# Dense layer of an attention, expert and dense kernel: the matmuls of its two products alternate in threes

## The chip, the cores and the metric

The kernel runs on one core of a Trainium2 chip. The metric is the device time of one execution in microseconds (us), as the median of several runs. The core has a matrix engine (TensorE, "PE" in the profile, with its weight loads as "PEld"), a vector engine (VectorE, "DVE"), a scalar engine (ScalarE, "ACT"), GpSimd ("POOL") and a queue that starts DMAs (SyncE, "SP"). Each engine runs its own instructions in program order and waits on semaphores for the others.

## The reference

The kernel computes three layers after one another; only the last one is touched by the change.

```python
def reference(**kwargs):
    ...
    attn_out = _attn_ref(**attn_kwargs)          # clustered attention
    ...
    x = _moe_ref(x=x, **moe_kwargs)              # 1536 tokens, one of 8 experts each
    return _moe2_ref(x=x, **moe2_kwargs)         # the dense layer

def _moe2_ref(x, w_in, w_out) -> np.ndarray:
    h = x @ w_in                                 # (1536, 512) @ (512, 2048)
    g = h * (1.0 / (1.0 + np.exp(-1.702 * h)))
    return (g @ w_out).astype(np.float32)        # (1536, 2048) @ (2048, 512)
```

## The kernel before

Attention fills the first 280 us, the experts the time up to about 490 us, the dense layer the rest. Every operand of the dense layer is held as a high and a low part, and each product of two blocks is made of three matmuls: high by high, high by low, low by high.

The dense layer is cut into 48 groups, numbered `g` in the list `seq`. A group is one block of 128 hidden columns for one block of 512 tokens. The order is: two halves of the hidden columns (`fh`), three token blocks (`tb`) in each, eight groups in each of these. Two products belong to a group:

- The first product, here called in(g), is the function `dense_in`. It runs over four slices `k` of the 512 model columns with three matmuls each (L1084, L1085, L1086). All twelve matmuls have 512 columns and add into one PSUM buffer `ph` (there are four of them, `ps_h`). The moving operands are `yth` and `ytl`, the experts' results; the weights come from `w`.
- The second product, here called out(g), is `dense_out`. It runs over four blocks `m` of 128 model columns with three matmuls each (L1176 and L1177 read `gh`, L1178 reads `gl`), 512 columns wide, and adds into four PSUM buffers `py`, one for each `m`, which stay open over eight groups.

Between the two, `dense_h` makes g out of h: ACT takes the sigmoid of `ph` into `sg` (L1160), DVE multiplies (L1161), ACT rounds to the high part `gh` (L1164) and DVE subtracts to get the low part `gl` (L1167). There are three buffers each of `gh` and `gl`, and one `sg`.

The order of the instructions is written out by hand (`tc.manual_schedule`). The last loop of the kernel makes one step for each g. A step issues, in this order: the twelve matmuls of in(g); the sigmoid and the multiply of g; the twelve matmuls of out(g-2), block by block; after the last group of eight, `dense_store` for each block (an ACT copy L1183 in the first half, a DVE add L1185 and an output DMA from POOL in the second); the rounding to `gh`; two pieces of `dense_step`; the subtraction to `gl`; the remaining pieces of `dense_step`. `dense_step` converts the weights of later groups from 64-bit to two parts: L842 and L857 on ACT, L843, L846, L849, L852 on DVE, L858 on POOL. in(0) has already been issued in the experts' loop. So TensorE starts the layer with in(1), in(2), out(0), in(3), out(1).

Of the kernel before, what the change touches and what calls it, by code (L numbers as in the profile page):

```python
# [9 lines left out]
F32 = mybir.dt.float32  # L10
# [35 lines left out]
def attention_moe_ffn(ctx: ExitStack, tc: tile.TileContext, q, k, v, centroids, w_gate, w_og, w1, w2, w_in, w_out, out):  # L46
# [3 lines left out]
    def f32(ap):  # L50
        return ap.bitcast(F32)
# [14 lines left out]
    def scatter_id(b, j):  # L66
        x = nc.gpsimd.indirect_dma_start(
            out=idd[:, :], out_offset=bass.IndirectOffsetOnAxis(ap=ci[:, b, j:j + 1], axis=0),
            in_=tok[:, b, j:j + 1], in_offset=None).ins
        nc.gpsimd.engine_nop()  # L70
        tc.declare_no_dep(x, group="ids", reason="every token has a place of its own")
        tc.add_to_no_dep_group("ids", x)
        ids.append(x.name)
# [604 lines left out]
    def place_ids():  # L678

        nc.vector.tensor_tensor(eoff, off, ebase, op=ALU.subtract)  # L680
        for b in range(B):
            t1 = const.tile([128, T, E], F32, name=f"t1{b}")
            t2 = const.tile([128, T], F32, name=f"t2{b}")
            nc.vector.tensor_tensor(t1, roh[b], eoff[:, None, :].to_broadcast([128, T, E]), op=ALU.mult)
            nc.vector.tensor_reduce(t2, t1, op=ALU.add, axis=AX.X)
            nc.vector.tensor_tensor(ci[:, b], t2, place[b], op=ALU.add)
# [80 lines left out]
    def need(x, names):  # L767
        for nm in names:
            tc.add_manual_dep(x, nm, DATA_DEP, reason="all of them scattered")
# [7 lines left out]
    ps_h = ctx.enter_context(tc.tile_pool(name="ps_h", reuse_waits="tile", bufs=4, space=PSUM))  # L777
# [84 lines left out]
    def wa(key, part, k, i):  # L862
        return pairs[key]["w", 0][:, part].rearrange("p (k f) -> p k f", k=4)[:, k, i * 128:(i + 1) * 128]
# [54 lines left out]
    def win_h(d, key, i, defer=False):  # L918
        n = d["n"]
        ph = ps_h.tile([128, 512], F32, name="ph", tag="ph")  # L920
        for k in range(4):
            product(ph, n, wa(key, 0, k, i), wa(key, 1, k, i), d["t"][:, k], k == 0, k == 3)
        ht = hp.tile([128, 2 * CAP], F32R, name="ht", tag="ht")[:, :2 * n]
        lo, hi = ht[:, 0:n], ht[:, n:]
        t = ph[:, :n]
        if n <= 256:

            total(ph, n, t)
        nc.scalar.activation(hi, t, AF.Relu)

        def rest():
            nc.vector.scalar_tensor_tensor(lo, t, 0.0, f32(hi), op0=ALU.max, op1=ALU.subtract)
        if defer:
            return ht, rest
        rest()
        return ht
# [117 lines left out]
    def dense_step(upto):  # L1054
        while dl["done"] < min(upto, 20 * (DFF // 256)):
            if dl["done"] % (20 // QN) == 0:
                c, g = units[dl["split"]]
                dl["split"] += 1
                if wide:
                    new = wide_stages(c, g)  # L1060
                    if todo:
                        todo.appendleft(new.pop(0))
                    todo.extend(new)
                else:
                    todo.append(lambda: split_pair(("d", 0, c), g, dense_pool(c)))
                    todo.extend([None] * 9)
            f = todo.popleft()
            if f:
                f()
            dl["done"] += 1  # L1070
            if dl["done"] % (20 // QN) == 0:
                dense_load(dl["split"] + 2)


    seq = [(fh, tb, c, i) for fh in range(2) for tb in range(NT // 512) for c in range(4 * fh, 4 * fh + 4) for i in range(2)]
    ahead = {}

    def dense_in(g):
        _, tb, c, i = seq[g]
        key = ("d", 0, c)  # L1080
        ph = ps_h.tile([128, 512], F32, name="ph", tag="ph")
        cs = slice(tb * 512, tb * 512 + 512)
        for k in range(4):
            nc.tensor.matmul(ph, wa(key, 0, k, i), yth[:, k, cs], start=(k == 0), stop=False)  # L1084
            nc.tensor.matmul(ph, wa(key, 0, k, i), ytl[:, k, cs], start=False, stop=False)  # L1085
            nc.tensor.matmul(ph, wa(key, 1, k, i), yth[:, k, cs], start=False, stop=(k == 3))  # L1086
        ahead[g] = ph

    with tc.manual_schedule():
        win_start(0, True)  # L1090
# [22 lines left out]
        for g in range(G + 2):  # L1113
# [10 lines left out]
            if g < G:  # L1124
                ht, low = win_h(wins[e], ("e", e, c // 2), c % 2, True)
                hq.append((g, ht))
            if g == G + 1:
                dense_in(0)
            if g >= 2:
                g0, ht = hq.popleft()  # L1130
# [25 lines left out]
    def dense_h(ph):  # L1156
        gh = gp.tile([128, 512], F32R, name="gh", tag="gh")
        gl = gp.tile([128, 512], F32R, name="gl", tag="gl")
        sg = gp.tile([128, 512], F32, name="sg", tag="sg", bufs=1)
        nc.scalar.activation(sg, ph, AF.Sigmoid, scale=1.702)  # L1160
        nc.vector.tensor_tensor(sg, ph, sg, op=ALU.mult)  # L1161

        def high():
            nc.scalar.copy(gh, sg)  # L1164

        def low():
            nc.vector.tensor_tensor(gl, sg, f32(gh), op=ALU.subtract)  # L1167
        return gh, gl, high, low
# [3 lines left out]
    def dense_out(m, key, i, gh, gl, first, last):  # L1172
        if first:
            po[m] = ps_y.tile([128, 512], F32, name=f"py{m}", tag=f"py{m}")
        ms = slice(m * 128, (m + 1) * 128)
        nc.tensor.matmul(po[m], gh[:, ms], wb(key, 0, i), start=first, stop=False)  # L1176
        nc.tensor.matmul(po[m], gh[:, ms], wb(key, 1, i), start=False, stop=False)  # L1177
        nc.tensor.matmul(po[m], gl[:, ms], wb(key, 0, i), start=False, stop=last)  # L1178

    def dense_store(m, fh, tb):  # L1180
        t = tb * 4 + m
        if fh == 0:
            nc.scalar.copy(acc[t], po[m])  # L1183
            return
        nc.vector.tensor_tensor(acc[t], po[m], acc[t], op=ALU.add)  # L1185
        x = nc.gpsimd.indirect_dma_start(  # L1186
            out=out, out_offset=bass.IndirectOffsetOnAxis(ap=idxc[:, t:t + 1], axis=0),
            in_=acc[t], in_offset=None).ins
        nc.gpsimd.engine_nop()
        tc.declare_no_dep(x, group="outs", reason="every token has a row of its own")  # L1190
        tc.add_to_no_dep_group("outs", x)
# [3 lines left out]
    with tc.manual_schedule():  # L1195
        gq = deque()
        for g in range(len(seq) + 2):
            high = low = None
            if g < len(seq):
                if g not in ahead:  # L1200
                    dense_in(g)
                gh, gl, high, low = dense_h(ahead.pop(g))
                gq.append((g, gh, gl))
            if g >= 2:

                for m in range(4) if g < len(seq) or g == len(seq) + 1 else ():
                    for g0, gh, gl in list(gq)[:1] if g < len(seq) else gq:
                        fh, tb, c, i = seq[g0]
                        dense_out(m, ("d", 0, c), i, gh, gl, g0 % 8 == 0, g0 % 8 == 7)
                    if g0 % 8 == 7:  # L1210
                        dense_store(m, fh, tb)
                if g < len(seq):
                    gq.popleft()
            if high:
                high()
            if g == IDS - 1:
                place_ids()
            if IDS <= g < IDS + B * T:
                scatter_id((g - IDS) // T, (g - IDS) % T)
            if g == IDS + B * T:  # L1220
                x = nc.sync.dma_start(out=idxc, in_=idd.rearrange("(t p) o -> p (t o)", p=128)).ins
                need(x, ids)
            upto = min(80, 52 + 6 * g) if g < 6 else min(120, 80 + 3 * (g - 5)) if g < 20 else 120 + 4 * (g - 19)
            dense_step(min(upto, dl["done"] + 2))
            if low:
                low()
            dense_step(upto)
# [28 lines left out]
```

## Time and profile before

| what | value |
|---|---|
| median of 3 runs | 758.22 us (757.78 to 758.63) |
| the profiled execution's own time | 760.4 us |
| its span, first to last instruction | 758.7 us |
| its mean granted TensorE clock | 0.981 of full speed |
| TensorE matmuls busy | 727.9 us, 96% |
| VectorE busy | 509.2 us, 67% |
| ScalarE busy | 421.7 us, 56% |
| GpSimd busy | 269.9 us, 36% |

A matmul's row in the timeline shows when it starts and for how long it is in the engine. Matmuls are pipelined: the next one starts while the last one is still draining, so the rate is read from the distance of two starts and not from the duration. A busy share of 100% says only that no gap is left between the rows, not that the rows can't be closer. A bracket at a row's end gives the engine's idle time before it and what ended it.

### The profile page before, as it was taken

The page shows a single profiled execution, that of the slowest core. Times are in us where ns is not written, and L with a number is a line of the kernel's source. Part 1 is how long each engine was busy: PE and PEld are TensorE (multiplying, and loading weights), DVE is VectorE, ACT ScalarE, POOL GpSimd, SP SyncE. Part 2 cuts the span into 40 slices and gives each one's busy share as a digit, 9 for nine tenths or more (in the row PEclk, how much of TensorE's full clock was granted, in tenths as well). Part 3 has the DMA queues.
Part 4 walks back from the last instruction along what each step waited for, and adds up shares of the span by engine and source line. Part 5 has one row for each costly group of instructions (what it writes and reads, how often), then busy time and mean ns, then how long its engine had stood idle before and what let it go on. Part 6 is the DMA issues. An engine that isn't in the chain of part 4 may idle for free. (4 is left out here: it accounts for less than half of the span.)

```text
span 758.7 us, 12232 instructions
## 1 busy us (share of the span) xinstructions
PE 727.9 (96%) x4285; PEld 650.6 (86%) x4286; DVE 509.2 (67%) x1000; ACT 421.7 (56%) x873; POOL 269.9 (36%) x212
## 2 busy tenths in 40 slices
PE   7999999999999977999999998999999999999996
PEld 5899999899899967999989888877888888888885
DVE  6798898989989983444676666797655466332322
ACT  3787777877767853555767766545434344212220
POOL 4111131111752022756778888332333122020202
PEclk8899999999999997999999999999999999999999
DMA  8847649457260027766657766133444221010101
GB/s 224 172 139 195 191 143 281 124 107 169 75 175 10 2 65 260 254 221 224 220 169 250 240 233 222 57 111 111 57 55 58 57 82 55 1 56 0 56 1 55
DMA packets 66240, 98.23 MB, mean 129 GB/s; under 512 B 9248, under 2 KB 44960, under 8 KB 66176
## 3 DMA queue, kind: packets, MB, share of 16 engines
q1 hardware_dynamic: 63872, 91.12, 42.3%
q0 software_dynamic: 2304, 6.30, 2.2%
q8 instruction: 35, 0.57, 0.3%
q14 instruction: 29, 0.24, 0.1%
HBM read 64.46 MB, written 12.59 MB: 102 GB/s over the span
## 5 line engine op out<-in xcount | busy, mean ns | idle before, releaser
L811 POOL TENSOR_TENSOR w<-raw,w 128x1024 fp32r<-128x1024 f32 x47 | 117.6, 2516 | 36.1 <-ACT w L808 20.3
L461 ACT CAST pth<-pt 128x384 fp32r<-128x384 f32 x192 | 83.7, 483 | 50.3 <-PE pt L457 47.8
L462 DVE TENSOR_TENSOR ptl<-pt,pth 128x384 fp32r<-128x384 f32 x192 | 97.5, 545 | 19.3 <-ACT pth L461 18.9
L1161 DVE TENSOR_TENSOR sg<-ph,sg 128x512 f32<-128x512 f32 x48 | 33.2, 691 | 102.2 <-ACT sg L1160 96.6
L443 DVE TENSOR_REDUCE nm<-sp 128x1 f32<-128x768 f32 x96 | 90.8, 946 | 4.3 <-PE sp L441 4.3
L858 POOL TENSOR_TENSOR w<-csq,w 128x512 fp32r<-128x512 f32 x32 | 43.5, 1359 | 138.6 <-ACT w L857 135.8
L449 ACT ACTIVATE P<-sp,nm 128x768 f32<-128x768 f32 x96 | 88.0, 916 | 3.2 <-DVE nm L443 3.0
L1160 ACT ACTIVATE sg<-ph 128x512 f32<-128x512 f32 x48 | 28.6, 596 | 108.5 <-PE ph L1086 102.8
L457 PE MATMUL pt<-ident,P 128*128 128x128 f32 x576 | 80.6, 274 | 1.9 <-DVE ptl L462 1.9
L1085 PE MATMUL ph<-ytl,w 128*128 128x512 f32 x192 | 76.2, 397 | 0.0
L1084 PE MATMUL ph<-yth,w 128*128 128x512 f32 x192 | 75.9, 395 | 0.0
L1178 PE MATMUL py<-w,gl 128*128 128x512 f32 x192 | 75.0, 391 | 0.5 <-DVE gl L1167 0.5
L1086 PE MATMUL ph<-yth,w 128*128 128x512 f32 x192 | 75.5, 393 | 0.0
L457 PEld LDWEIGHTS pt<-ident,P 128*128 128x128 f32 x576 | 67.8, 140 | 8.8 <-DVE ptl L462 5.5
L440 PE MATMUL sp<-X,Q 128*128 128x384 f32 x192 | 74.1, 386 | 1.3 <-DMA X<-Lk 1.3
L1177 PE MATMUL py<-w,gh 128*128 128x512 f32 x192 | 75.3, 392 | 0.0
L1176 PE MATMUL py<-w,gh 128*128 128x512 f32 x192 | 75.0, 391 | 0.0
L808 ACT CAST w<-raw 128x1024 fp32r<-128x1024 f32 x64 | 66.8, 1044 | 7.5 <-DMA raw<-in_moe_w_dram 6.6
L479 PE MATMUL po<-pth,vst 128*128 128x384 f32 x192 | 69.7, 363 | 0.0
L441 PE MATMUL sp<-Z,Q 80*128 80x384 f32 x192 | 66.7, 348 | 1.7 <-DMA Q<-ohT 1.4
L908 PE MATMUL py<-ht,w 128*128 128x480 f32 (+5 forms) x192 | 61.2, 352 | 6.8 <-DVE room L915 4.6
L480 PE MATMUL po<-ptl,vst 128*128 128x384 f32 x192 | 64.9, 338 | 0.0
(241 smaller groups left out, 1702.3 us busy)
## 6 DMA issues: line engine op xcount, KB each, us to landing
raw<-in_moe_w_dram SPq DMA_DIRECT2D x64, 512.0 KB, 3.9
raw<-in_moe_w_in_dram SPq DMA_DIRECT2D x16, 512.0 KB, 5.5
raw<-in_moe_w_out_dram SPq DMA_DIRECT2D x16, 512.0 KB, 3.4
Q<-Hq SPq DMA_DIRECT2D x32, 192.0 KB, 6.2
xd<-zrow SPq DMA_DIRECT2D x8, 768.0 KB, 7.0
ld_q<-in_q_dram SPq DMA_DIRECT2D x8, 384.0 KB, 4.0
ld_k<-in_k_dram SPq DMA_DIRECT2D x8, 384.0 KB, 3.9
ld_v<-in_v_dram SPq DMA_DIRECT2D x8, 384.0 KB, 7.0
```

The source lines that it names most:

```text
L443: nc.vector.tensor_reduce(nm, sp[:, :, :384], op=ALU.max, axis=AX.XY, negate=True)
L449: nc.scalar.activation(P, L["sp"][:, :, :384], AF.Exp, bias=L["nm"], accum_out=L["sm"][:, j % 3:j % 3 + 1])
L457: nc.tensor.transpose(pt[:, r * 128:(r + 1) * 128], L["P"][:, n, r * 128:(r + 1) * 128], ident)
L461: nc.scalar.copy(hi, src)
L462: nc.vector.tensor_tensor(L["ptl"][:, 3 * n:3 * n + 3, qs], src, f32(hi), op=ALU.subtract)
L811: (eng or nc.gpsimd).tensor_tensor(lo, r, f32(hi), op=ALU.subtract)
L1084: nc.tensor.matmul(ph, wa(key, 0, k, i), yth[:, k, cs], start=(k == 0), stop=False)
L1085: nc.tensor.matmul(ph, wa(key, 0, k, i), ytl[:, k, cs], start=False, stop=False)
L1086: nc.tensor.matmul(ph, wa(key, 1, k, i), yth[:, k, cs], start=False, stop=(k == 3))
L1176: nc.tensor.matmul(po[m], gh[:, ms], wb(key, 0, i), start=first, stop=False)
L1177: nc.tensor.matmul(po[m], gh[:, ms], wb(key, 1, i), start=False, stop=False)
L1178: nc.tensor.matmul(po[m], gl[:, ms], wb(key, 0, i), start=False, stop=last)
```

## The change

`dense_in` gets a list of slices, so that one slice of three matmuls can be issued alone. In the steps g = 2 to 46 ("mixed") the loop over the four blocks `m` now issues slice k = m of in(g) and then block m of out(g-2): three matmuls of the first product, three of the second, and so on. In these steps `dense_h` for g comes after that loop, since `ph` is complete only then, and so also after the stores. The steps 0, 1 and 47 and the end stay as they were. No instruction is added or removed: PE has 3811 rows in its listing in both kernels.

```diff
-    def dense_in(g):
+    def dense_in(g, ks=range(4)):
...
-        for k in range(4):
+        for k in ks:
             nc.tensor.matmul(ph, wa(key, 0, k, i), yth[:, k, cs], start=(k == 0), stop=False)
             nc.tensor.matmul(ph, wa(key, 0, k, i), ytl[:, k, cs], start=False, stop=False)
             nc.tensor.matmul(ph, wa(key, 1, k, i), yth[:, k, cs], start=False, stop=(k == 3))
...
+            outs = list(gq) if g == len(seq) + 1 else list(gq)[:1] if 2 <= g < len(seq) else []
+            mixed = 2 <= g < len(seq) - 1
+
+            def start():
+                ph = dense_h(ahead.pop(g))
+                gq.append((g, *ph[:2]))
+                return ph[2:]
+            if g < len(seq) and not mixed:
                 if g not in ahead:
                     dense_in(g)
-                gh, gl, high, low = dense_h(ahead.pop(g))
-                gq.append((g, gh, gl))
...
+                high, low = start()
+            if outs:
+                for m in range(4):
+                    if mixed:
+                        dense_in(g, (m,))
+                    for g0, gh, gl in outs:
                         fh, tb, c, i = seq[g0]
                         dense_out(m, ("d", 0, c), i, gh, gl, g0 % 8 == 0, g0 % 8 == 7)
                     if g0 % 8 == 7:
                         dense_store(m, fh, tb)
...
+            if mixed:
+                high, low = start()
```

The lines of the changed kernel are numbered one to three higher: L1086 to L1088 for the first product, L1177 to L1179 for the second, L1161 and L1165 for sigmoid and rounding.

The first place is TensorE's queue at out(0), the first block of the second product. Before, the end of in(2) and the first block of out(0):

```order
L1084 MATMUL ph<-yth,w_6024 128x512
L1085 MATMUL ph<-ytl,w_6024 128x512
L1086 MATMUL ph<-yth,w_6024 128x512
L1176 MATMUL py_7096<-w_5481,gh 128x512
L1177 MATMUL py_7096<-w_5481,gh 128x512
L1178 MATMUL py_7096<-w_5481,gl 128x512
L1176 MATMUL py_7100<-w_5481,gh 128x512
```

And now, from the first slice of in(2) on:

```order
L1086 MATMUL ph<-yth,w_6024 128x512
L1087 MATMUL ph<-ytl,w_6024 128x512
L1088 MATMUL ph<-yth,w_6024 128x512
L1177 MATMUL py_7082<-w_5481,gh 128x512
L1178 MATMUL py_7082<-w_5481,gh 128x512
L1179 MATMUL py_7082<-w_5481,gl 128x512
L1086 MATMUL ph<-yth,w_6024 128x512
L1087 MATMUL ph<-ytl,w_6024 128x512
L1088 MATMUL ph<-yth,w_6024 128x512
L1177 MATMUL py_7089<-w_5481,gh 128x512
```

Before, all twelve matmuls of in(2) stood ahead of the first matmul that reads `gl`; now three of them do, and the other nine come behind it.

The second place is ScalarE's queue in the step of the first store. Before, the sigmoid of g = 9 stands ahead of the four copies of out(7):

```order
L1160 ACTIVATE sg<-ph 128x512
L1183 COPY acc_7012<-py_7096 128x512
L1183 COPY acc_7013<-py_7100 128x512
L1183 COPY acc_7014<-py_7104 128x512
L1183 COPY acc_7015<-py_7108 128x512
L1164 CAST gh<-sg 128x512
```

Now it stands behind them:

```order
L1184 COPY acc_7012<-py_7082 128x512
L1184 COPY acc_7013<-py_7089 128x512
L1184 COPY acc_7014<-py_7096 128x512
L1184 COPY acc_7015<-py_7103 128x512
L1161 ACTIVATE sg<-ph 128x512
L1165 CAST gh<-sg 128x512
```

The sigmoid has moved past the four copies; in a step without stores the orders of ACT and DVE are what they were.

## Rows read from the trace of the kernel before

**Rows 1.** Page, part 1: busy us, share of the span and instructions of each engine
```profile
PE 727.9 (96%) x4285; PEld 650.6 (86%) x4286; DVE 509.2 (67%) x1000; ACT 421.7 (56%) x873; POOL 269.9 (36%) x212
```
**Rows 2.** Windows: length, busy PE PEld DVE ACT POOL (instructions), PEclk, DMA share, GB/s
```profile
295.90:302.30 6.40, 6.40 (x29) 5.62 (x28) 2.05 (x4) 3.98 (x7) 2.19 (x1) 0.50 1.03 354
...
488.50:523.20 34.70, 34.16 (x148) 27.12 (x146) 28.11 (x44) 17.01 (x31) 9.68 (x7) 1.00 0.29 102
523.20:741.40 218.20, 218.20 (x947) 177.87 (x947) 105.16 (x162) 75.21 (x127) 43.08 (x37) 1.00 0.22 46
```
**Rows 3.** Waits of PE from 486 to 752: us in total, times, longest
```profile
PE py L1178 <- DVE gl L1167: 0.5, 1, 0.5
```
**Rows 4.** Timeline of PE, one steady step: start us, duration us, engine, line, operation, tiles
```profile
724.85 0.39 PE L1084 MATMUL ph<-yth,w 128*128 128x512 f32 x1
...
725.53 0.40 PE L1084 MATMUL ph<-yth,w 128*128 128x512 f32 x1
...
727.64 0.39 PE L1176 MATMUL py<-w,gh 128*128 128x512 f32 x1
...
728.80 0.39 PE L1178 MATMUL py<-w,gl 128*128 128x512 f32 x1
...
730.38 0.39 PE L1084 MATMUL ph<-yth,w 128*128 128x512 f32 x1
```
**Rows 5.** Timeline of PE at the layer's start: in(1), in(2), first of out(0)
```profile
488.52 0.40 PE L1084 MATMUL ph<-yth,w 128*128 128x512 f32 x1
...
491.31 0.39 PE L1084 MATMUL ph<-yth,w 128*128 128x512 f32 x1
...
494.09 0.39 PE L1176 MATMUL py<-w,gh 128*128 128x512 f32 x1
494.32 0.40 PE L1177 MATMUL py<-w,gh 128*128 128x512 f32 x1
495.25 0.51 PE L1178 MATMUL py<-w,gl 128*128 128x512 f32 x1 [0.54 <-DVE gl L1167]
```
**Rows 6.** Timeline of PE: first of out(3), first gl matmul of out(5), first of in(47)
```profile
511.56 0.39 PE L1176 MATMUL py<-w,gh 128*128 128x512 f32 x1
...
523.21 0.50 PE L1178 MATMUL py<-w,gl 128*128 128x512 f32 x1
...
741.45 0.39 PE L1084 MATMUL ph<-yth,w 128*128 128x512 f32 x1
```
**Rows 7.** Timelines of DVE and ACT: gl of groups 0 and 5, sigmoid of group 5
```profile
494.51 0.69 DVE L1167 TENSOR_TENSOR gl<-sg,gh 128x512 fp32r<-128x512 f32 x1
...
519.93 0.58 ACT L1160 ACTIVATE sg<-ph 128x512 f32<-128x512 f32 x1
...
522.47 0.68 DVE L1167 TENSOR_TENSOR gl<-sg,gh 128x512 fp32r<-128x512 f32 x1
```
**Rows 8.** Timelines of ACT, DVE and PE: sigmoid, copies, gl, gl matmul of step 25
```profile
622.77 0.60 ACT L1160 ACTIVATE sg<-ph 128x512 f32<-128x512 f32 x1 [1.09 <-PE ph L1086]
623.40 2.64 ACT L1183 COPY acc<-py 128x512 f32<-128x512 f32 x4
...
626.59 0.69 DVE L1167 TENSOR_TENSOR gl<-sg,gh 128x512 fp32r<-128x512 f32 x1 [1.44 <-ACT gh L1164]
...
634.04 0.39 PE L1178 MATMUL py<-w,gl 128*128 128x512 f32 x1
```
**Rows 9.** Timeline of PE, first expert: its second product, first product, second again
```profile
305.34 0.31 PE L904 MATMUL py<-ht,w 128*128 128x320 f32 x1
...
307.10 0.31 PE L904 MATMUL ph<-t,w 128*128 128x320 f32 x1
...
308.86 0.31 PE L904 MATMUL py<-ht,w 128*128 128x320 f32 x1
```
**Rows 10.** Timeline of PE: two long waits ahead of the experts
```profile
280.98 0.19 PE L557 MATMUL prk<-roh,tri 128*128 128x24 bf16 x1 [1.94 <-DVE roh L538]
...
291.48 1.65 PE L1099 MATMUL ph<-identb 128*128 128x128 bf16 x20 [2.34 <-issue]
```

More of the change, by code (lines that the diff above doesn't have):

```diff
@@ L1076, in attention_moe_ffn @@
     ahead = {}
-    def dense_in(g):
+    def dense_in(g, ks=range(4)):
         _, tb, c, i = seq[g]
         key = ("d", 0, c)
-        ph = ps_h.tile([128, 512], F32, name="ph", tag="ph")
+        if g not in ahead:
+            ahead[g] = ps_h.tile([128, 512], F32, name="ph", tag="ph")
+        ph = ahead[g]
         cs = slice(tb * 512, tb * 512 + 512)
-        for k in range(4):
+        for k in ks:
             nc.tensor.matmul(ph, wa(key, 0, k, i), yth[:, k, cs], start=(k == 0), stop=False)
@@ L1086, in dense_in @@
             nc.tensor.matmul(ph, wa(key, 1, k, i), yth[:, k, cs], start=False, stop=(k == 3))
-        ahead[g] = ph
     with tc.manual_schedule():
@@ L1198, in attention_moe_ffn @@
             high = low = None
-            if g < len(seq):
+            outs = list(gq) if g == len(seq) + 1 else list(gq)[:1] if 2 <= g < len(seq) else []
[5 more added lines that the diff above has]
+            if g < len(seq) and not mixed:
                 if g not in ahead:
                     dense_in(g)
-                gh, gl, high, low = dense_h(ahead.pop(g))
-                gq.append((g, gh, gl))
-            if g >= 2:
-                for m in range(4) if g < len(seq) or g == len(seq) + 1 else ():
-                    for g0, gh, gl in list(gq)[:1] if g < len(seq) else gq:
+                high, low = start()
[4 more added lines that the diff above has]
+                    for g0, gh, gl in outs:
                         fh, tb, c, i = seq[g0]
```

## The prediction

> **What bounds the kernel now.** I read the page's busy times first: TensorE's rows cover 96% of the span, VectorE's 67% [rows 1]. The windows say where that holds: from 523.2 to 741.4 us, most of the dense layer, TensorE has no gap at all, at full granted clock, while VectorE, ScalarE and GpSimd are busy for less than half of it [rows 2]. The waits of TensorE in the layer are one, of 0.54 us, for `gl` [rows 3]. So in the steady steps nothing can be gained from a wait; only the distance of two matmul starts can move. That distance is the next thing to read, from the starts in the timeline.
>
> In a steady step [rows 4] in(g) runs from 724.85 to 727.64 and out(g-2) from there to 730.38, 24 matmuls in 5.53 us. They are not even. The first three of in(g) take 0.68 us, 227 ns each. The other nine take 2.11 us, 234 ns each. The first five of out(g-2) take 1.16 us, 232 ns each, the other seven 1.58 us, 226 ns each. All have the same 512 columns and the same clock. At the layer's start 24 matmuls of the first product run in one go, from 488.52 to 494.09: 232 ns each, slow throughout [rows 5]. So there are two paces, some 227 and 232 to 234 ns. Long runs of the first product end in the slow one, long runs of the second in the fast one, and after a switch the old pace goes on for three to five matmuls. The changed order never lets a run get longer than three. What that does to the pace is the open question of this change; the waits can be worked out.
>
> **The wait at out(0).** Before, out(0) starts at 494.09 after all of in(2); its third matmul, which reads `gl`, could start at 494.55 and starts at 495.25 [rows 5], since VectorE has `gl` only at 494.51 + 0.69 = 495.20 [rows 7]. VectorE and ScalarE issue the steps 0 and 1 as they did, so `gl` comes no sooner. Now only three matmuls of in(2) stand ahead of out(0). TensorE comes to the reader of `gl` at 491.31 + 5 x 0.23 = 492.46 and waits 2.8 us instead of 0.7. The nine matmuls that used to cover the wait come after it: 9 x 232 = 2.09 us more.
>
> **The next steps give nothing back.** From the first reader of `gl` in out(0) to the one in out(5) there are 120 matmuls before and now: five whole steps. The reader in out(5) starts at 523.21 [rows 6], 0.05 us after its `gl` ends, 522.47 + 0.68 = 523.15 [rows 7]. A quicker TensorE would only wait there. Nor does this `gl` come later: before, in(5) is done when out(3) starts at 511.56 [rows 6], and its sigmoid runs only at 519.93 [rows 7], since ScalarE and VectorE are behind with converting weights. In the new order the last matmul of in(g) lies 15 behind the `gl` reader of out(g-2) where it lay 3 ahead of it, 18 matmuls or 4.2 us later; 515.8 is still ahead of 519.93. So the time until 523.21 stays, and from there to in(47) at 741.45 TensorE has 19 + 39 x 24 = 955 matmuls to run, where it had 946 in 218.24 us [rows 6].
>
> **Steady steps, waits.** `gl` of group 25, in a step with stores, is ready at 626.59 + 0.69 = 627.28 and read at 634.04 [rows 8]: 6.8 us to spare. The 4.2 us by which in(g) ends later come off, 2.6 us stay. The sigmoid is now behind the four store copies; three of them run while the loop is still going, and the fourth adds one copy and three matmuls, about 1.3 us, but the four copies (2.64 us [rows 8]) no longer stand between sigmoid and rounding. I take zero. If that cover were gone, each such step would lose what is missing; there are five mixed steps with stores, so a shortfall of 0.3 us would be 1.5 us. What is queued behind a later sigmoid on ScalarE and VectorE are the weight conversions; VectorE has half its time free [rows 2], and the weights of a later half are ready many steps ahead. The weights of the second product are not needed earlier, since the readers of out(g) keep their distance from one another. The end, from in(47) on, is issued as before.
>
> **The pace.** The rows give bounds. All 955 matmuls at the fast pace: 955 x 0.2267 = 216.5, with the longer start after the wait at 523.21 (its row is 0.50 long, others 0.39: 0.11 us [rows 4, 6]) 216.6, which is 1.6 us less than 218.24. All at the pace of the long run of the first product: 955 x 0.2321 + 0.1 = 221.8, or 3.5 us more; at the 234 ns of the nine it would be 5.7 us more. Rows for an alternation in threes at 512 columns do not exist. The nearest are the steady paces of the two products, 232.1 [rows 5] and 226.7 [rows 4], and half of the matmuls are of each kind. I take their mean, 229.4: 955 x 0.2294 + 0.1 = 219.2, which is 1.0 us more than 218.24. It is also about the middle of the bounds. It contains the nine matmuls of the wait: 2.1 us for these and 1.1 us back from the steadier pace.
>
> **Sum.** +1.0 us on the profiled execution (760.4 us, span 758.7). That one lies 0.3% over the median of the runs, 758.22, which changes a difference of this size by nothing. 759.2 us. A measurement tells about 0.2% of this kernel, 1.5 us, from no change, so this is "within".
>
> **Rivals.**
>
> *Short runs stay fast.* Three matmuls of the first product after a run of the second go at 227 ns in the steady step [rows 4], and the fourth is the first slow one. Now there is no fourth. If a slow pace never begins, 1.6 us are saved: 756.6. Against it: the second product needs five to recover, and gets three. It just reaches the edge of 0.2%.
>
> *The order has no say.* If each matmul keeps the pace that its product has on average, only the nine matmuls behind the wait count: +2.1, 760.3 us. For it: the first expert's twelve matmuls of the second product (305.34 to 307.10) and of the first (to 308.86) both take 147 ns at 320 columns, so runs into one PSUM buffer are not slow as such [rows 9]. Against it: L1084 alone shows two paces in one step [rows 4]. [...]
>
> *The slow pace stays: slower than before.* The slow state is there when the mixed steps begin, after 24 matmuls of the first product and a wait. If leaving it takes five matmuls of the second product in a row, as 727.64 to 728.80 suggests [rows 4], three are never enough, and all run at 232.1: +3.5, 761.8 us. It decides from the point where three matmuls of the second product do not undo three of the first.
>
> *The longer wait costs the clock.* TensorE now stands for 2.8 us in two pieces, the second about 2.1. A wait of 1.94 us left the clock full, one of 2.34 us [rows 10] was followed by a stretch at half the clock, 6.4 us of it in one window [rows 2]. At half the clock such a stretch loses about 3.2 us: 762.4. [...]
>
> **Chances.** Forecast (mean pace) 0.34; order has no say 0.22; short runs fast 0.25; slow pace stays 0.15; clock 0.04. Faster by over 0.2% (under 756.7): half of the short-run case and a little of the forecast's lower side, 0.18. Slower by over 0.2% (over 759.7): the second, fourth and fifth case and a fifth of the forecast's, some of the second falling short, 0.42. Within: the rest, 0.40. The forecast's own range is 757.9 to 760.3. The range for eight in ten takes in the short-run case with some error of its own and the slow case: 756.2 to 762.0.
>
> **What would show it.** In the profile after: the wait of the first L1179 on `gl` at about 492.5 to 495.3, ended by DVE's `gl`; the `gl` reader of out(5) still at 523.2; no other wait of TensorE; and the length of a steady step, 24 matmuls: 5.44 us if short runs stay fast, 5.51 by the forecast, 5.54 if the order has no say, 5.57 if the slow pace stays. in(47) then starts at 742.4. The prediction is wrong if waits for `gl` show up in the steady steps, if the reader in out(5) moves, or if the pace lies outside 227 to 234 ns.

## The result, and the profile after

The changed kernel took 762.77 us (median of 7 runs, 761.42 to 765.38), the kernel before 758.53 us (7 runs, 755.41 to 760.26). The ratio is 1.0061, 95% interval 1.0047 to 1.0075: slower by 0.6%. Measured again with the last experiments, it was 762.13 against 758.83 us, ratio 1.0040 (1.0024 to 1.0057). The forecast was 759.2 us, no change that can be told, with 762.0 as the upper end; the changed kernel lies above that end, and neither interval takes in a ratio of 1. Two later runs of the kernel before, of 888 and 1011 us at a mean granted clock of 0.75 and 0.65, are left out of the medians below.

Page of the changed kernel, part 1, to be held against [rows 1]:

```profile
PE 727.1 (96%) x4285; PEld 647.9 (85%) x4286; DVE 507.2 (67%) x1000; ACT 421.9 (56%) x873; POOL 270.1 (36%) x212
```

The busy sums tell little here: the same numbers of instructions, times within 3 us of before, PE even 0.8 us less. The windows of the changed kernel (length, busy time of PE, PEld, DVE, ACT, POOL with instructions, PEclk, DMA share, GB/s) answer to [rows 2]:

```profile
488.00:520.70 32.70, 30.35 (x130) 23.97 (x129) 27.22 (x41) 15.35 (x28) 8.39 (x6) 1.00 0.29 97
520.70:740.00 219.30, 219.30 (x947) 177.43 (x947) 104.04 (x161) 74.23 (x125) 43.27 (x37) 1.00 0.22 46
```

The first window has lost busy time of TensorE (30.35 of 32.70 us, before 34.16 of 34.70): that is the longer wait. In the second, TensorE has no gap, as before, and the clock is full in both; yet 947 matmul records take 219.30 us where they took 218.20. Waits of PE from 484 to 754 us (total, times, longest), against [rows 3]:

```profile
PE py L1179 <- DVE gl L1168: 1.7, 1, 1.7
PE py L1177 <- ACT gh L1165: 0.6, 1, 0.6
```

There are two, both at out(0), and none in a steady step. Timeline of PE in the changed kernel: first of in(2), the two waits, the first `gl` reader of out(5), first of in(47); compare [rows 5, 6]:

```profile
489.15 0.39 PE L1086 MATMUL ph<-yth,w 128*128 128x512 f32 x1
...
490.61 0.50 PE L1177 MATMUL py<-w,gh 128*128 128x512 f32 x1 [0.61 <-ACT gh L1165]
...
493.09 0.50 PE L1179 MATMUL py<-w,gl 128*128 128x512 f32 x1 [1.74 <-DVE gl L1168]
...
521.05 0.50 PE L1179 MATMUL py<-w,gl 128*128 128x512 f32 x1
...
742.42 0.39 PE L1086 MATMUL ph<-yth,w 128*128 128x512 f32 x1
```

Times are best counted from the start of in(2), since the part ahead of the dense layer differs by some microseconds from one execution to the next (in(1) began between 484.0 and 489.3 us in the 13 profiles of this study; the mean is 486.9 in the 8 with the plain order and 486.8 in the 5 with the alternation, so that part has no share in the loss that the profiles show).

| from, to | before | after |
|---|---|---|
| in(2) to the first `gl` reader of out(0) | 3.94 | 3.94 |
| to the one of out(5) | 31.90 | 31.90 |
| from there to in(47) | 218.24 (946 matmuls, 230.7 ns each) | 221.37 (955 matmuls, 231.8 ns each) |
| in(2) to in(47) | 250.14 | 253.27 |

The whole +3.13 us (0.41%) lies behind the reader of out(5): nine more matmuls there, 9 x 0.231 = 2.08 us, and 955 x 1.1 ns = 1.05 us because each is a little slower. One steady step of the changed kernel in the timeline of PE, the first of each three:

```profile
725.04 0.40 PE L1177 MATMUL py<-w,gh 128*128 128x512 f32 x1
...
725.74 0.39 PE L1086 MATMUL ph<-yth,w 128*128 128x512 f32 x1
...
726.42 0.39 PE L1177 MATMUL py<-w,gh 128*128 128x512 f32 x1
...
727.10 0.40 PE L1086 MATMUL ph<-yth,w 128*128 128x512 f32 x1
...
727.80 0.40 PE L1177 MATMUL py<-w,gh 128*128 128x512 f32 x1
...
728.50 0.39 PE L1086 MATMUL ph<-yth,w 128*128 128x512 f32 x1
...
729.19 0.40 PE L1177 MATMUL py<-w,gh 128*128 128x512 f32 x1
...
729.90 0.39 PE L1086 MATMUL ph<-yth,w 128*128 128x512 f32 x1
...
730.60 0.40 PE L1177 MATMUL py<-w,gh 128*128 128x512 f32 x1
```

From 725.04 to 730.60 it is 5.56 us, before 5.53 [rows 4]. The step does not run at one pace. The three of in(g) that begin at 725.74 and the three of out(g-2) at 726.42 take 0.68 us each; all other threes take 0.69 to 0.71. The six quick ones are slice 0 of in(g) and the output block 0 that follows. So a slow pace does not simply "go on": it is left, once a step, in a run of three, at slice 0, and it is back at slice 1. That is not what any of my rivals describes, and it is what the experiments follow up.

### The profile page after: what moved, and what is told of

It is laid out like the page before. It is cut to its first block, busy times and chain, and to the rows that moved or that the text cites. A ratio compares the mean times of both kernels' runs of the same rounds, so it can differ in the third digit from the quotient of the medians.

```text
span 759.6 us, 12229 instructions
## 1 busy us (share of the span) xinstructions
PE 727.1 (96%) x4285; PEld 647.9 (85%) x4286; DVE 507.2 (67%) x1000; ACT 421.9 (56%) x873; POOL 270.1 (36%) x212
## 5 line engine op out<-in xcount | busy, mean ns | idle before, releaser
L1161 ACT ACTIVATE sg<-ph 128x512 f32<-128x512 f32 x48 | 28.7, 598 | 103.8 <-PE ph L1088 96.0
L1179 PE MATMUL py<-w,gl 128*128 128x512 f32 x192 | 75.8, 395 | 1.7 <-DVE gl L1168 1.7
L1177 PE MATMUL py<-w,gh 128*128 128x512 f32 x192 | 75.8, 395 | 0.6 <-ACT gh L1165 0.6
L1086 PE MATMUL ph<-yth,w 128*128 128x512 f32 x192 | 75.5, 393 | 0.0
L1088 PE MATMUL ph<-yth,w 128*128 128x512 f32 x192 | 75.4, 393 | 0.0
```

## The experiments

Two readings stood at the start. **P**, position: the pace follows the length of the run of one product (the forecast's reading). **S**, what is read: something in slices 1 to 3 themselves is slow, in the moving operand or in the weights. All distances of matmul starts below are read from the timeline of PE; the kernel before has, from a switch on, 227, 226, 227, 237, 235, 232, 233, 241, 232, 236, 235, 233 ns in the first product and 226, 236, 228, 233, 231, then seven of 226 to 227 in the second.

### Slices in reverse

```
-        for k in range(4):
+        for k in (3, 2, 1, 0):
```

(`start` and `stop` go with the new first and last slice.)

> The kernel before with the four slices of in(g) in the order 3, 2, 1, 0. Theory S (what is read): matmuls that read the slices 1 to 3 of the first product's operands are slow, and a few behind them; then the first three matmuls of in(g) start slow at once, some 235 ns, and the second product is back at 227 ns sooner than its sixth matmul; a step near 5.53 us or a little under. Theory P (position): the first three matmuls after a run of the second product are fast whatever they read; then the starts are as in the kernel before, three at 227, nine at 234, and a step of 5.53 us. The whole within 1.5 us of before by both.

Measured: 760.81 us (one run), step 5.527 us. The first product now begins 234, 233, 233, 232, 228, 230 ns: right after five quick matmuls of the second product, its first one is slow. Timeline of PE, the first of slice 3 and, three matmuls later, the first of slice 2:

```profile
725.31 0.39 PE L1084 MATMUL ph<-yth,w 128*128 128x512 f32 x1
...
726.01 0.39 PE L1084 MATMUL ph<-yth,w 128*128 128x512 f32 x1
```

These three take 0.70 us; before, the first three of a step took 0.68 [rows 4]. P falls, S stands. Two things missed. The second product did not recover sooner: its first seven matmuls are slow (it was five), and so are the three of slice 0, which are now the last of the first product. And the whole is 2.9 us over the median of the kernel before, not within 1.5; from in(2) to in(47) it is only 0.66 us more (250.80 against 250.14), about as much as one step lost to a new wait:

```profile
515.64 0.50 PE L1086 MATMUL ph<-yth,w 128*128 128x512 f32 x1 [0.63 <-POOL w L858]
```

The reversed order asks for a half of the weights that GpSimd had not yet converted; this is not a matter of pace. The rest of the 2.9 us lies outside the dense part, and one run does not settle it.

### All moving operands from slice 0

```
-            nc.tensor.matmul(ph, wa(key, 0, k, i), yth[:, k, cs], ...
+            nc.tensor.matmul(ph, wa(key, 0, k, i), yth[:, 0, cs], ...
```

(and the same for the other two lines of the three)

> The kernel before, but all twelve matmuls of in(g) take their moving operand from slice 0 of yth and ytl (the slices 1 to 3 of the experts' results are left out of the sum; weights as before). Theory S with the moving operand as the cause: no slow pace is left, 24 matmuls in 5.44 us, 46 steps x 0.10 = 4 to 5 us less than before, some 754. Theory S with the weights as the cause, and theory P: 5.53 us a step, time as before.

### All weights from slice 0

```
-            nc.tensor.matmul(ph, wa(key, 0, k, i), yth[:, k, cs], ...
+            nc.tensor.matmul(ph, wa(key, 0, 0, i), yth[:, k, cs], ...
```

> The kernel before, but all twelve matmuls of in(g) take their weights from slice 0 (the weights of the slices 1 to 3 are left out; moving operand as before). Theory S with the weights as the cause: 5.44 us a step, 4 to 5 us less than before. Theory S with the moving operand, and theory P: 5.53 us a step, time as before.

Measured: with the moving operands of slice 0, 757.41 us (one run) and every matmul of a steady step at 226 or 227 ns, step 5.440 us. With the weights of slice 0, 755.84 us (one run), step 5.533 us, and the pattern of before, matmul for matmul. (Of single runs the step and not the time counts: I had expected some 754 us for the first, and its dense part is indeed 3.58 us shorter, 246.56 from in(2) to in(47), but not its whole time.) Timeline of PE in these two, the first `gl` reader of out(5) and the first matmul of in(47), 946 matmuls later. Moving operands from slice 0:

```profile
524.00 0.50 PE L1178 MATMUL py<-w,gl 128*128 128x512 f32 x1
...
738.55 0.39 PE L1084 MATMUL ph<-yth,w 128*128 128x512 f32 x1
```

Weights from slice 0:

```profile
518.70 0.50 PE L1178 MATMUL py<-w,gl 128*128 128x512 f32 x1
...
736.91 0.39 PE L1084 MATMUL ph<-yth,w 128*128 128x512 f32 x1
```

214.55 us against 218.21: 226.8 and 230.7 ns. It is the moving operand's slice that costs. The second product's matmuls become quick with it, though nothing in them was changed: a slow matmul of the first product delays some that follow it (before, the first five of out(g-2), at 226 to 236 ns).

### Alternation only from group 8 on

```
-            mixed = 2 <= g < len(seq) - 1
+            mixed = 8 <= g < len(seq) - 1
```

> The changed kernel with the mixed steps only from g = 8 on. If the loss has two parts, nine matmuls moved behind the wait at out(0) (2.1 us) and the pace of the mixed steps (5.560 against 5.537 us, 0.02 us for each), the first part goes: the wait on gl at out(0) is 0.5 us as before, from in(2) to in(47) it takes 250.1 + 39 x 0.023 = 251.0 us, and the whole is 0.9 us slower than before (759.4). If instead the order in threes costs the loss by itself, it stays 3 us slower or more.

Measured: 760.34 us (median of 10 runs), against 757.92 for the kernel before, ratio 1.0036 (1.002 to 1.0052). From in(2) to in(47) 251.91 us, 1.77 more than before and 1.36 less than the changed kernel. I had expected 251.0 us, with the loss from the nine matmuls gone. The alternating steps behind the first take 5.560 us, which is 39 x 0.027 = 1.05 us of the 1.77; nearly all of the other 0.72 us lies in the first alternating step, of 6.34 us. So both parts of the loss are there, and starting later gives back 1.36 of the nine matmuls' 2.08 us. The waits of PE say why it is not all of it (total, times, longest):

```profile
PE py L1179 <- DVE gl L1168: 0.9, 2, 0.5
```

There is a second short wait for `gl`, of 0.37 us at out(6), in the step in which the alternation sets in: its `gl` comes too late once nine matmuls that stood before its reader stand behind it.

### Why slices 1 to 3? Their addresses

`yth` and `ytl` hold four slices of 1808 columns, 7232 bytes, per partition. 7232 = 28 x 256 + 64: slices 1, 2 and 3 begin 64, 128 and 192 bytes off slice 0, modulo 256. By the built program's tile addresses slice 0 of `yth` (115808) and of `ytl` (144736), the blocks of `w`, `gh` and `gl` that these matmuls read all begin at 96 modulo 256. (In the second product `w` is the moving operand, and `gh` or `gl` are the weights.) So the second product and slice 0 read moving operand and weights at the same place modulo 256, slices 1 to 3 do not. Theory A: that is what costs. Theory B: slice 0 is quick for another reason.

Slice 0 shifted by 16 columns (64 bytes) and by 32 columns (128 bytes), on top of the kernel with all moving operands from slice 0:

```
-        cs = slice(tb * 512, tb * 512 + 512)
+        c0 = min(tb, 1) * 512 + 16
+        cs = slice(c0, c0 + 512)
```

> The kernel before, with the moving operand of every matmul of the first product read from slice 0 and 16 columns (64 bytes) further on; it leaves out slices 1 to 3 and computes something else. Theory A, that a moving operand is slow by where its address stands against the others' (slices 1 to 3 begin 64, 128 and 192 bytes off slice 0, modulo 256): all twelve matmuls of the first product at 230 to 237 ns start to start, step at least 5.55 us, against 5.440 us with the same slice at offset 0. Theory B, that slice 0 is fast because it is slice 0, wherever its columns begin: step 5.440 us, all matmuls 226 to 227 ns.

> As the kernel with 16 columns, but 32 columns (128 bytes) further on. Theory A with a period of 128 bytes: step 5.440 us. Theory A with a period of 256 bytes or more: at least 5.55 us (slice 2 of the kernel before stands 128 bytes off, and its matmuls took 228 to 241 ns). Theory B: 5.440 us.

Measured: 757.95 and 759.31 us (one run each), steps 5.533 and 5.527 us, against 5.440 us with the same slice unshifted. B falls. Timeline of PE with 16 columns, `gl` reader of out(5) and first of in(47), 218.20 us for 946 matmuls as in the kernel before, though all twelve now read slice 0:

```profile
520.80 0.50 PE L1179 MATMUL py<-w,gl 128*128 128x512 f32 x1
...
739.00 0.40 PE L1085 MATMUL ph<-yth,w 128*128 128x512 f32 x1
```

The pattern at 64 bytes is 237, 235, 231, 232, 226, 229, 232, 225, 230, 231, 226, 229 ns, and the first ten matmuls of the second product behind it are at 224 to 236 too; at 128 bytes it alternates, 237 and 229, and the second product is quick from its fourth matmul on. I had expected 230 to 237 for all twelve and a step of at least 5.55 us; the direction is right, the size is 0.02 us off. Twelve shifted matmuls cost a step no more than the nine of the kernel before (5.533 us), so the loss does not go by their number. Where slice 0 of `ytl` in the kernel before stands 256 bytes off that of `yth` modulo 512 (144736 - 115808 = 113 x 256), nothing is lost (226 to 227 ns), and at 64, 128 and 192 bytes there is a loss (234 to 235 ns on average over each of the slices 1 to 3); if it goes by a period, that is 256 bytes.

Then the cure: slices of 1792 columns, 7168 bytes, 28 x 256.

```
-YC = NT + max(CAPS[1:])
+YC = NT + 256
...
-... LEAST + (e0 - 1) * ((NT - LEAST) // (E - 1)), NT, ...
+... LEAST + (e0 - 1) * ((NT - LEAST) // (E - 1)), min(NT, YC - CAPS[e0]), ...
```

The room behind the 1536 tokens shrinks from 272 to 256 columns. Only the second expert has a window of 272, so this form serves inputs of which the first expert takes at most 1520 of 1536 tokens; a general one would need 48 columns more instead of 16 fewer.

> The kernel before with slices of 1792 columns (7168 bytes, 14 times 512) in place of 1808 (7232 bytes), so that all four slices begin at the same place modulo 512 bytes; nothing else moves on an engine. Theory A: steady step 5.440 us in place of 5.533, from the first steady step on; from in(2) to in(47) 250.14 less some 40 x 0.093 = 3.7, about 246.4 us; median about 754, faster by 0.4 to 0.6%. Theory B: step 5.533 us, time the same within 0.2%.

> The changed kernel with slices of 7168 bytes. Theory A: steady step 5.440 us in place of 5.560, so the order of the matmuls has no say in the pace; from in(2) to in(47) 253.27 less some 42 x 0.12 = 5.0, about 248.2 us, which is 1.5 to 2 us more than the kernel before with the same slices, all of it the longer wait at the first y; median 756 to 757. Theory B: step 5.560 us, median about 762.

Measured: the kernel before with such slices 754.82 us (8 runs) against 758.44 for the kernel before (17 runs), ratio 0.9951 (0.9933 to 0.997); the changed one with such slices 757.97 us (12 runs), ratio to the kernel before 0.9988 (0.9974 to 1.0002). Both have a step of 5.440 us and not one matmul in a steady step outside 226 to 227 ns. From in(2) to in(47) it is 246.55 us, as expected (246.4), and 248.59 us for the changed order, a little more than the 248.2 expected; that kernel's median is 1 us over the 756 to 757 expected. Timeline of PE, `gl` reader of out(5) and first of in(47), for the order of before:

```profile
519.87 0.50 PE L1178 MATMUL py<-w,gl 128*128 128x512 f32 x1
...
734.43 0.39 PE L1084 MATMUL ph<-yth,w 128*128 128x512 f32 x1
```

and for the changed order:

```profile
523.68 0.50 PE L1179 MATMUL py<-w,gl 128*128 128x512 f32 x1
...
740.28 0.39 PE L1086 MATMUL ph<-yth,w 128*128 128x512 f32 x1
```

214.56 us for 946 matmuls and 216.60 for 955, both 226.8 ns each. The difference is 2.04 us, and nine matmuls at 226.8 ns are 2.04. With the slices in line the order has no say in the pace, and what is left of the change's loss is the nine matmuls.

### Is it the address itself, or how the operands stand to each other?

The kernel before with slices of 7168 bytes, and a tile of 64 bytes ahead of all others:

```
+    first = const.tile([128, 16], F32, name="first")
+    nc.gpsimd.memset(first, 0.0)
     idxc = const.tile([128, NT // 128], I32, name="idxc")
```

> The kernel before with slices of 7168 bytes, and a tile of 64 bytes allocated ahead of all others, so that weights, slices and gh, gl all begin 64 bytes further on (160 in place of 96 modulo 256) while they stand to each other as before. Theory A1, that a matmul is slow when its moving operand and its weights begin at different places modulo 256 bytes: steady step 5.440 us, all matmuls 226 to 227 ns. Theory A2, that the address by itself is slow (96 modulo 256 is fast, 160 and 224 are not): about 229 to 232 ns each, step 5.5 us or more.

Measured: 754.33 us (one run), step 5.440 us, all matmuls at 226 or 227 ns. The same two rows of PE's timeline, 214.56 us apart:

```profile
520.94 0.50 PE L1180 MATMUL py<-w,gl 128*128 128x512 f32 x1
...
735.50 0.39 PE L1086 MATMUL ph<-yth,w 128*128 128x512 f32 x1
```

At 160 modulo 256 slices are quick when weights stand there too (226.8 ns); in the shifted slice above, 160 against weights at 96 was slow (225 to 237 ns, 230 on average). So it is the relation. The weights alone were never moved, and which part of a matmul or of the weight load running beside it suffers was not told apart.

### Both losses taken away, the alternation kept

The changed kernel with slices of 7168 bytes, alternating from group 16 on:

```
-            mixed = 2 <= g < len(seq) - 1
+            mixed = 16 <= g < len(seq) - 1
```

> The changed kernel with slices of 7168 bytes and the alternation only from group 16 on, where no gl is late. Theory: with the pace out of play, the whole loss of the changed order is the nine matmuls behind the early wait; so step 5.440 us throughout, no wait beyond the 0.7 us at the first y, and from in(2) to in(47) 246.5 us, as the kernel before with such slices (246.55), against 248.59 with the alternation from group 2; time within 0.1% of the 754.8 us of that kernel. Rival: the alternation itself costs something that only shows with it (the turn from product to product, or a gl that comes late at group 16): 247.5 us or more.

Measured: 754.45 us (4 runs), against 758.83 for the kernel before, ratio 0.9923 (0.9897 to 0.995). From in(2) to in(47) 246.58 us (246.55 with the order of before and such slices). Its only wait of PE in the dense part is the one that the order of before has:

```profile
PE py L1179 <- DVE gl L1168: 0.7, 1, 0.7
```

With the operands in line, turning from product to product every three matmuls costs nothing by itself. This kernel and the order of before with such slices (754.82 us) cannot be told apart, and both beat the kernels before and after.

### The changed kernel once more

> The changed kernel once more, unchanged, for a narrower interval: the traces give 3.13 us more in the dense part (0.41%); the first comparison gave 0.61% with 0.47% as its lower end. If all of the loss lies in the dense part: ratio near 1.0041 and an interval that takes it in. If something outside it costs another 1 us: ratio 1.0055 or more again.

Measured: 762.13 us (7 runs) against 758.83 (12 runs), ratio 1.0040 (1.0024 to 1.0057). From in(2) to in(47) 253.26 us, 0.01 from the first profile. The 3.13 us of the dense part are 0.41%; this interval takes them in, the first one (from 0.47% on) missed them by 0.06%. The medians of the alternating kernels lie 0.2 to 1.1 us further from those of the plain ones than the traces explain (for the pair with slices of 7168 bytes 3.15 against 2.03 us). Some 0.2 us of that lies outside the span from first to last instruction: the time of a run less its span is about 1.7 us for every kernel in the plain order and, in the median, 1.9 to 2.0 us for every alternating one. For the rest the profiles show no place, and I leave it open; it is not more than the runs of one kernel differ among themselves.

## Why the prediction was wrong

**The wait at out(0): right.** TensorE was to wait 2.8 us in place of 0.7; it waits 0.61 us for `gh` and 1.74 us for `gl`, and each of the two first matmuls after a wait is 0.1 us longer. From the start of in(2) to that reader it is 3.94 us, and five matmuls at 0.23 leave 2.8 of it, as forecast. I had named only `gl`; that `gh` is late as well changes nothing, since `gl` comes after it. `gl` came no sooner: its reader starts 3.94 us after in(2) in the kernel before too.

**Nothing given back until out(5): right, to 0.01 us.** The timeline of DVE of the changed kernel has the `gl` of group 5 here:

```profile
520.31 0.68 DVE L1168 TENSOR_TENSOR gl<-sg,gh 128x512 fp32r<-128x512 f32 x1
```

It ends at 520.99 and is read at 521.05, as before [rows 7]. So the nine matmuls that no longer cover the wait are paid in full: 2.04 us in the pair with slices in line.

**No waits in the steady steps, full clock: right.** No wait beyond the two stands in the list, and PEclk is 1.00 in both windows. That a wait in two pieces might cost the clock fell. But one reading behind that rival was wrong: the wait of 1.94 us [rows 10] did not leave the clock full. In the trace of the kernel before PEclk is 0.50 from 282.10 to 285.30 us, beginning about 1 us after that wait ended. Both waits were followed by a stretch at half the clock (behind the one of 2.34 us, PEclk is 0.50 from 292.50 to 302.30 us), and TensorE did little around them (0.82 us of 3.00 between 278.50 and 281.50, 1.16 of 3.50 between 289.00 and 292.50); here it was busy for 30.35 of 32.70 us. So the length of the wait was not a safe sign either way.

**The pace: this is the step that failed.** The forecast took 229.4 ns per matmul, the mean of two steady paces, and so 219.2 us for the 955 matmuls; they took 221.37 us, 231.8 ns each. These 2.2 us are the whole difference between the forecast's +1.0 and the +3.13 of the traces. The size was wrong because the reading behind it was: I took the two paces for something that builds up in a long run of the first product and wears off in a long run of the second. Reversing the slices showed that the first matmul after a long run of the second product is slow too, if it reads slice 3. What costs is nine of the twelve matmuls of the first product, those whose moving operand stands elsewhere modulo 256 bytes than its weights; in every order that was run each three of them takes 0.69 us or more, against 0.68 in line, and what stands around them decides how many neighbours are slowed. Before, the last seven of the second product's twelve had only their like ahead of them and were quick, ten of 24 with slice 0. In threes, only slice 0 and the block behind it are, six of 24. The mean of the two products' paces was no bound and no estimate of that: the alternation keeps every cause and spreads its effect. How large the effect is does not follow from counting alone. Over the 5.440 us of a step in line, 14 slow matmuls lose 0.093 us before and 18 lose 0.120 in threes, but in the reversed order 19 lose only 0.087. By what rule the delay is passed on stays open.

**The rivals.** "The slow pace stays" gave 761.8 us and a step of 5.57; measured were a step of 5.560 and 231.8 ns, against its 232.1. Its +3.5 us is 0.4 off, and its reason is half right: behind slices 1 to 3, three matmuls of the second product are indeed too few to recover in, but the slow pace does not stay, it is left and entered anew in every step. "The order has no say" is true of a kernel whose operands stand in line (5.440 us in either order) and was not of this one: in the runs of this study a matmul of 512 columns starts 226.7 ns after the one before where the operands of all of them stand alike, and up to 14 ns later than that where they do not. The row that spoke for it, 147 ns in both products at 320 columns [rows 9], is of matmuls whose operands stand alike too: by the built program's addresses all of them begin at 96 modulo 256. "Short runs stay fast" rested on the three quick matmuls at the switch; they were quick because they read slice 0.

**What could have been seen.** [rows 4] showed exactly three quick matmuls at the start of in(g), and three is the number of matmuls of a slice; a pace that wears in has no reason to turn just there. What led away from it was the run of in(1) and in(2) in [rows 5], where slice 0 of in(2) is slow too (225, 236 and 229 ns). It stands right behind slice 3 of in(1), so it is slowed as the first five of out(g-2) are. (Slice 0 of in(1) is slow as well, and that is not explained: see the end.) The addresses of the slices could have been worked out from the tile's shape, 4 x 1808 columns, without any run.

## What to carry to other kernels

When one instruction with one shape runs at two speeds, line the speeds up with what each one reads before reading them as a history: which slice, which tile, which address modulo a power of two. Where a matmul's operands are slices of a larger tile, give the slices a length that keeps moving operand and weights at the same place modulo 256 bytes; here 64 bytes less per slice were worth 3.6 us of the dense part (24 matmuls in 5.440 in place of 5.533 us), 0.5% of the time, where the change in order cost 3.1 and could by my own bounds have gained 1.6. This is shown for float32 matmuls that each load their own weights, and for no others. And cover of a wait is counted at the wait: nine matmuls moved from before to behind it cost their full time, 2.04 us, since the thing waited for, and a later one like it, came no sooner.

## What was not expected of the hardware

In a steady step a float32 matmul of 128x512 with a weight load of its own starts 226.7 ns after the one before when moving operand and weights of all of them begin at the same place modulo 256 bytes, whether that is 96 or 160 (24 matmuls in 5.440 us in both). With the two 64, 128 or 192 bytes apart, starts in a steady step are 225 to 241 ns apart, 229 to 235 on average over a slice. The delay also falls on matmuls that follow and whose own operands stand alike: on three behind a shift of 128 bytes, on five behind slice 3 (192 bytes), on ten behind a shift of 64 bytes (slice 0 shifted: ten of the second product; slices in reverse, where slice 1 comes before slice 0: three of slice 0 and seven of the second product).

One place does not fit, and stays open. In both kernels with slices of 7168 bytes the first five matmuls of in(1) begin 233, 236, 228, 233 and 231 ns apart, and only then 226 to 227. They stand behind matmuls of the last expert with 320 and 256 columns, whose operands by the built program's addresses are in line too. So operands out of line are not the only thing that slows the matmuls that follow.
